# One decode step of cached attention with a gated unit: another order of the weight loads, and the key and value loads of the last pair in one piece

## The chip, the cores and the metric

The kernel runs on one core of a Trainium2 chip. The metric is the device time of one execution in microseconds; lower is better. Before the change the median of three runs is 687.23 us.

## The reference

Everything is float32. One token `x` of 512 elements is normalised, goes through an attention over 8192 cached positions with 32 heads of 128, and the result is multiplied by a gate made from the same normalised token:

```python
def _A_ref(x, k_cache, v_cache, wq, wo):
    q = (lambda x, *d: x.transpose(*d))((x @ wq).reshape(B, Sq, H, Dh), 0, 2, 1, 3)
    scores = jnp.einsum("bhqd,bhkd->bhqk", q, k_cache) * (Dh ** -0.5)
    p = _softmax(scores, axis=-1)
    o = jnp.einsum("bhqk,bhkd->bhqd", p, v_cache)
    return (lambda x, *d: x.transpose(*d))(o, 0, 2, 1, 3).reshape(B, Sq, H * Dh) @ wo
...
    g = jnp.einsum("bsd,df->bsf", x, w_gate)
    u = jnp.einsum("bsd,df->bsf", x, w_up)
    h = _sigmoid(g) * u
    return jnp.einsum("bsf,fd->bsd", h, w_down)
...
    xn = _layernorm(x, axis=-1)
    s = _A_ref(xn, A_k_cache, A_v_cache, A_wq, A_wo)
    g = _silu(_B_ref(xn, B_w_gate, B_w_up, B_w_down))
    return x + s * g
```

`wq` is 512x4096 (8.39 MB), `wo` 4096x512 (8.39 MB), `w_gate` and `w_up` 512x1376 (2.82 MB each), `w_down` 1376x512. The key cache and the value cache have 134 MB each. Every byte is used once, so the kernel is one long load with work beside it.

## The kernel before, in words

Three big buffers hold what is loaded: A, B and C (named slot_55, slot_56 and slot_57 in the built program, slot in the profile), each 128 partitions of 64 KB. The heads go in 16 pairs; the 64 upper partitions carry one head of a pair, the 64 lower ones the other. The keys of pair n, called Kn here, go to B for even n and to A for odd n. The values Vn go to C, except V15, which goes to B. One such load is 8.39 MB, with one row of 64 KB for each partition.

SP issues all the big loads, in the order of its program, and waits on semaphores between them. At the start (L145 to L153) come the gate weights, the up weights and the down weights into A, the last 96 rows of the down weights into `wd_rest`, the query weights into C, and K0 into B. ScalarE issues two small loads: `x_col`, the token as 128 rows of 16 bytes (L148), and `x_row` (L163).

Once `x_col` has landed, VectorE makes the normalised token `xn` (L185 to L199; two small matmuls on TensorE and a square root on ScalarE stand in between). Then, for the gate weights and after them the up weights (loop L211), VectorE multiplies the four slices with `xn` and adds them up (`weighted`, L203), and TensorE sums over the partitions and turns the result by 11 narrow matmuls (L216, L217); this is called a turn below. VectorE multiplies both (L224), does the same with the down weights (L227, L229), and TensorE sums them in four gate matmuls (L233), whose count is `n_gate`. ScalarE and VectorE make the gate row of it (L237, L239). VectorE then spreads `xn` into `xnb` (L240), which lies in the same memory as `wd_rest`, and TensorE computes the queries: eight tiles of four matmuls each, a loop of its own (L246 to L250), one tile to each of the eight PSUM banks; ScalarE copies each to `q_all` (L257).

From there on, for each pair: VectorE multiplies the keys with the query in place and reduces (`scores`, two halves, L277 and L279), the maximum goes through TensorE, ScalarE takes the exponentials into `prz` (`softmax`), and TensorE multiplies them with the values in 64 matmul records once these have landed (`pair`, L314). The waits of SP set when a load may start:

```python
    sp.wait_ge(s_pe.sem, n_gate)
    load_k(1)
...
    sp.wait_ge(s_q, nq)
    for n in range(NP - 1):
        if n:
            sp.wait_ge(s_po, n)
        sp.dma_start(C, rows_of(v_src, n)).then_inc(d_v, 16)
        if n + 2 < NP:
            sp.wait_ge(s_dve.sem, k_free[n])
```

So K1 (into A) waits for the gate matmuls, V0 (into C) for the last query tile, a later Vn for the matmuls with the values before it, and K(n+2) for the scores of pair n. K15 is loaded in two halves (L265), and so is V15 (L342, L343); `pair` waits for the second half of V15 in the middle of its matmuls. At the end `wo` goes to C in five pieces (L346), and TensorE projects (L364 to L389).

Of the kernel before, what the change touches and what calls it, by code (L numbers as in the profile page):

```python
# [9 lines left out]
P = 128  # L10
# [15 lines left out]
def kernel(  # L26
# [11 lines left out]
    nc = tc.nc  # L38
# [31 lines left out]

    A, B, C = (over(f"slot{i}", SLOT, SLOTS + i * SLOT * 4) for i in range(3))
    q_all = put("q_all", NP * Dh).rearrange("p (n d) -> p n d", d=Dh)
    wd_rest = put("o1", QT)
    o1 = wd_rest
    sc = [put("sc0", NB), put("sc1", NB)]
    ident = put("ident", P)
    ones = put("ones", P)
    prz = put("prz", NB * 2).rearrange("p (j a) -> p j a", a=2)
    x_row = put("x_row", GC)
    g_row = put("g_row", GC)  # L80
    heads = put("heads", NP * 4).rearrange("p (n c) -> p n c", c=4)
# [19 lines left out]
    wd_t = A[:, 2 * KT * F:2 * KT * F + FP * D].rearrange("p (r e) -> p r e", e=D)  # L101
    wq_t = C.rearrange("p (k c) -> p k c", k=KT)
    wo_t = C.rearrange("p (r e) -> p r e", e=D)
    late = SLOT // 2

    psum = nc.alloc_psum_tensor("psum", [P, 8 * QT], F32).ap()
    bank = [psum[:, i * QT:(i + 1) * QT] for i in range(8)]
    po, pt, pm, acc, fold_ps, o_ps, oTl = bank[0], bank[1], bank[2], bank[4], bank[5], bank[6], bank[7]


    sems = []
# [24 lines left out]
    k_sem = lambda n: d[f"k{n % 2}"]  # L136
    k_free = {}

    def rows_of(src, n, lo=0, hi=SLOT):
        return src[n * P:(n + 1) * P, lo:hi]  # L140


    xv = x.rearrange("a b d -> (a b d)")
    with tc.tile_critical(no_gpsimd_drain=True):
        d["wg"].by(sp.dma_start(wg_t, w_gate.rearrange("(p k) f -> p k f", k=KT)), 16)  # L145
    tc.close()
    tc.compile()
    d["x"].by(act.dma_start(x_col, xv.rearrange("(p k) -> p k", k=KT)), 16)  # L148
    d["wu"].by(sp.dma_start(wu_t, w_up.rearrange("(p k) f -> p k f", k=KT)), 16)
    d["wd"].by(sp.dma_start(wd_t, w_down[:FP * P, :].rearrange("(p r) e -> p r e", r=FP)), 16)  # L150
    d["wd"].by(sp.dma_start(wd_rest[:FL, :], w_down[FP * P:, :]), 16)
    d["wq"].by(sp.dma_start(wq_t, wq.rearrange("(p k) c -> p k c", k=KT)), 16)
    d["k0"].by(sp.dma_start(B, rows_of(k_src, 0)), 16)  # L153


# [5 lines left out]
    n_xrow = s_dve.by(dve.memset(ones, 1.0))  # L161
    act.wait_ge(s_dve.sem, n_xrow)
    d["xr"].by(act.dma_start(x_row[0:P:GP, :], xv.rearrange("(g c) -> g c", g=NG)), 16)  # L163
    dve.memset(st[:, 6:7], EPS)
    dve.memset(rs2, 0.0)
    dve.memset(prz.rearrange("p j a -> p (j a)"), 0.0)
    for b in (0, 5):
        dve.memset(bank[b], 0.0)
    for b, cols in ((1, GC), (4, GC), (6, FP + 1), (7, FP + 1)):
        dve.memset(bank[b][:, :cols], 0.0)  # L170
    dve.wait_ge(s_pool.sem, 2)
    for g in range(NG):
        n_set = s_dve.by(dve.tensor_copy(pick[g * GP:(g + 1) * GP, :], ident[g * GP:(g + 1) * GP, g * GP:g * GP + ROWS * 2]))
# [2 lines left out]
    def self_wait():  # L176
        dve.wait_ge(s_dve.sem, s_dve.n)
# [28 lines left out]
            self_wait()  # L206
            s_dve.by(dve.scalar_tensor_tensor(acc, t(k), col(k), acc, op0=ALU.mult, op1=ALU.add))  # L207

    turned = [bank[6 + a][:, :FP + 1] for a in range(2)]
    self_wait()  # L210
    for a, (name, t) in enumerate((("wg", wg_t), ("wu", wu_t))):  # L211
        dve.wait_ge(d[name].sem, 16)
        weighted(t[:, 0, :], lambda k: t[:, k, :], lambda k: xn[:, k:k + 1], KT)
        pe.wait_ge(s_dve.sem, s_dve.n)
        for i in range(FP):
            m = pe.matmul(turned[a][:, i:i + 1], t[:, 0, i:FP * P:FP], ones[:, 0:1], start=True, stop=True)  # L216
        m = pe.matmul(turned[a][:FL, FP:FP + 1], t[:, 0, FP * P:F], ones[:, 0:1], start=True, stop=True)  # L217
        n = s_pe.by(m)
        if a == 0:
            act.wait_ge(s_pe.sem, n)  # L220
            n_sg = s_act.by(act.activation(sg, turned[0], AF.Sigmoid))
    dve.wait_ge(s_act.sem, n_sg)
    dve.wait_ge(s_pe.sem, n)
    s_dve.by(dve.tensor_mul(hid, sg, turned[1]))  # L224
    self_wait()
    dve.wait_ge(d["wd"].sem, 32)
    weighted(wd_t[:, 0, :], lambda r: wd_t[:, r, :], lambda r: hid[:, r:r + 1], FP)  # L227
    self_wait()
    s_dve.by(dve.scalar_tensor_tensor(wd_t[:FL, 0, :], wd_rest[:FL, :], hid[:FL, FP:FP + 1], wd_t[:FL, 0, :],  # L229
                                      op0=ALU.mult, op1=ALU.add))  # L230
    pe.wait_ge(s_dve.sem, s_dve.n)
    for g in range(NG):
        m = pe.matmul(bank[1][g * GP:g * GP + 1, :GC], ones[:, 0:1], wd_t[:, 0, g * GC:(g + 1) * GC],  # L233
                      start=True, stop=True)
    n_gate = s_pe.by(m)
    act.wait_ge(s_pe.sem, n_gate)
    n = s_act.by(act.activation(g_row, bank[1][:, :GC], AF.Sigmoid))  # L237
    dve.wait_ge(s_act.sem, n)
    n_grow = s_dve.by(dve.tensor_mul(g_row, g_row, bank[1][:, :GC]))  # L239
    n_xnb = s_dve.by(dve.tensor_copy(xnb, xn.rearrange("p (k o) -> p k o", o=1).to_broadcast([P, KT, P])))  # L240


    pe.wait_ge(d["wq"].sem, 16)
    pe.wait_ge(s_dve.sem, n_xnb)
    nq = H // NG
    with nc.Fori(0, nq, engines=[pe.engine]) as t:  # L246
        for k in range(KT):
            m = pe.matmul(psum[:, bass.ds(t * QT, QT)], xnb[:, k, :], wq_t[:, k, bass.ds(t * QT, QT)],  # L248
                          start=(k == 0), stop=(k == KT - 1))
        m.then_inc(s_q, 1)  # L250
    n_qc = []
    for t in range(nq):
        act.wait_ge(s_q, t + 1)
        pairs = slice(t * NG // 2, (t + 1) * NG // 2)
        for a in range(2):
            r = slice(a * HALF, (a + 1) * HALF)
            c = act.copy(q_all[r, pairs, :], bank[t][r, :].rearrange("p (n a d) -> p n a d", a=2, d=Dh)[:, :, a, :])  # L257
        n_qc.append(s_act.by(c))


    def load_k(n, parts=1):
        w = SLOT // parts
        for i in range(parts):
            c = k_sem(n) if i == parts - 1 else d["ka"]
            c.by(sp.dma_start(k_slot(n)[:, i * w:(i + 1) * w], rows_of(k_src, n, i * w, (i + 1) * w)), 16)  # L265


    def scores(n, waits):
        kt = k_slot(n).rearrange("p (j d) -> p j d", d=Dh)
        s = sc[n % 2]  # L270
        h = NB // 2
        q = q_all[:, n:n + 1, :].to_broadcast([P, h, Dh])
        for i in range(2):
            if waits[i] is not None:
                dve.wait_ge(*waits[i])
            part = kt[:, i * h:(i + 1) * h, :]
            s_dve.by(dve.tensor_mul(part, part, q))  # L277
# [21 lines left out]
        s_act.by(act.copy(heads[:, n, :], oTl[:, 0:4]))  # L299


    def pair(v, waits):
        take(pe, s_rm)
        pe.matmul(pt[:1, :P], mx[:, 0:1], ident, start=True, stop=True).then_inc(s_pt, 1)  # L304
        take(pe, s_am)
        pe.matmul(pm[:, 0:2], ones[:1, :], mx[:1, 2:4], start=True, stop=True).then_inc(s_pm, 1)  # L306
        take(pe, s_pr)
        pe.matmul(oTl[:, 2:4], ones, rs2, start=True, stop=True)  # L308
        nj = NB // ROWS
        for j in range(nj):  # L310
# [3 lines left out]
            m = pe.matmul(po[g * GP:g * GP + 2 * ROWS, :], prz[:, j * ROWS:(j + 1) * ROWS, :],  # L314
                          v[:, j * QT:(j + 1) * QT], start=(j < NG), stop=(j >= nj - NG))
        m.then_inc(s_po, 1)
        take(pe, s_o1)
        for b in range(ROWS):
            m = pe.matmul(oTl[:, 0:2], o1[:, b * Dh:(b + 1) * Dh], pick[:, 2 * b:2 * b + 2],  # L319
                          start=(b == 0), stop=(b == ROWS - 1))  # L320
        m.then_inc(s_ot, 1)
# [3 lines left out]
    for n in range(NP):  # L325
        if n % (NG // 2) == 0:
            dve.wait_ge(s_act.sem, n_qc[n // (NG // 2)])
        if n < NP - 1:
            scores(n, ((k_sem(n).sem, 16 * (n // 2 + 1)), None))
        else:  # L330
            scores(n, ((d["ka"].sem, 16), (k_sem(n).sem, 16 * (n // 2 + 1))))
        softmax(n)
    sp.wait_ge(s_q, nq)
    for n in range(NP - 1):
# [2 lines left out]
        sp.dma_start(C, rows_of(v_src, n)).then_inc(d_v, 16)  # L337
# [5 lines left out]
    d["vb"].by(sp.dma_start(B[:, late:], rows_of(v_src, NP - 1, late, SLOT)), 16)  # L343
# [87 lines left out]
```

## Time and profile before

| | |
|---|---|
| three runs | 687.17, 687.23, 688.38 us |
| the profiled execution, own time | 686.93 us |
| its span, first to last instruction | 685.0 us |
| VectorE busy | 588.8 us (86%) |
| TensorE matmul busy | 241.1 us (35%) |
| ScalarE busy | 41.5 us (6%) |
| read from memory | 293.67 MB |

The profiled execution's time is 1.9 us more than its span, and 0.3 us under the median of the runs. In the profile PE is TensorE, PEld its weight loads, DVE VectorE, ACT ScalarE, POOL GpSimd, SP SyncE; a q behind a name stands for that engine's sequencer. q1 is the DMA queue that SP issues to, q10 the one of ScalarE. L numbers are lines of the kernel before. A matmul in float32 leaves two records, so that 11 matmuls are 22 of them.

### The profile page before, as it was taken

The numbers are of one execution on the slowest core, as the hardware profiler recorded it, in microseconds if no ns is written. First come the engines' busy times: TensorE is split into PE (matmuls) and PEld (weight loads), VectorE is DVE, ScalarE is ACT, GpSimd is POOL, SyncE is SP. The second block draws the span as 40 slices with busy tenths as digits, with TensorE's granted clock in tenths as the row PEclk, the third lists the DMA queues.
The fourth block names the chain that finished last, engine by engine and source line by source line (L and its number), as shares of the span: only waits on it lengthen the run. The fifth ranks groups of instructions, "written<-read, shape, count | busy, mean of one in ns | idle before, by whom it ended". The sixth has DMA issues, their size and how long they took to land. (4 is left out here: it accounts for less than half of the span.)

```text
span 685.0 us, 3539 instructions
## 1 busy us (share of the span) xinstructions
PE 241.1 (35%) x1490; PEld 90.4 (13%) x1490; DVE 588.8 (86%) x147; ACT 41.5 (6%) x135; POOL 0.7 (0%) x6
## 2 busy tenths in 40 slices
PE   0549306060503305050422406060422406060465
PEld 0514101010101101010110101010110101010022
DVE  2643999999999999999989899898979899899930
ACT  1002010000000000000010100000010100000010
POOL 0000000000000000000000000000000000000000
PEclk9999756575665657575565657565565756565689
DMA  9999999999999999999999999999999999999997
GB/s 365 435 429 429 438 425 444 440 432 436 437 432 432 432 429 429 436 444 436 432 436 436 432 432 432 429 429 436 444 436 432 436 436 432 432 419 442 423 430 313
DMA packets 6469, 293.74 MB, mean 429 GB/s; under 512 B 856, under 2 KB 864, under 8 KB 1216
## 3 DMA queue, kind: packets, MB, share of 16 engines
q1 hardware_dynamic: 6312, 293.67, 99.3%
q8 instruction: 3, 0.05, 0.0%
q10 hardware_dynamic: 152, 0.00, 0.0%
q14 instruction: 2, 0.02, 0.0%
HBM read 293.67 MB, written 0.00 MB: 429 GB/s over the span
## 5 line engine op out<-in xcount | busy, mean ns | idle before, releaser
L277 DVE TENSOR_TENSOR slot<-slot,q_all 128x8192 f32<-128x8192 f32 x32 | 277.8, 8681 | 36.7 <-DMA slot<-in_A_k_cache_dram 36.7
L279 DVE TENSOR_REDUCE sc<-slot 128x64 f32<-128x8192 f32 x32 | 278.0, 8686 | 1.1
L314 PE MATMUL psum<-slot,prz 128*8 128x512 f32 x1024 | 147.6, 741 | 214.1 <-PEq L131 214.1
L314 PEld LDWEIGHTS psum<-slot,prz 128*8 128x8 f32 x1024 | 30.1, 103 | 317.9 <-issue 317.9
L304 PE MATMUL psum<-ident,mx 128*1 128x128 f32 x32 | 9.1, 387 | 147.7 <-PEq L131 147.7
L297 ACT COPY o<-psum 128x512 f32<-128x512 f32 x16 | 9.4, 586 | 373.9 <-PE psum L314 373.9
L248 PE MATMUL psum<-slot,o 128*128 x64 | 30.4, 639 | 1.4 <-DVE o L240 1.4
L304 PEld LDWEIGHTS psum<-ident,mx 128*1 128x1 f32 x32 | 1.8, 80 | 149.3 <-issue 149.3
L319 PE MATMUL psum<-pick,o 128*128 128x2 f32 x128 | 16.4, 250 | 12.8 <-PEq L131 12.8
L319 PEld LDWEIGHTS psum<-pick,o 128*128 128x128 f32 x128 | 15.5, 191 | 27.2 <-issue 27.2
L308 PE MATMUL psum<-rs,ones 128*128 128x2 f32 x32 | 8.9, 349 | 23.4 <-PEq L131 23.4
L248 PEld LDWEIGHTS psum<-slot,o 128*128 128x128 f32 x64 | 13.0, 206 | 18.4 <-issue 18.4
L284 DVE TENSOR_REDUCE mx<-psum 1x2 f32<-1x128 f32 x16 | 4.4, 278 | 12.1 <-PE psum L304 12.1
L293 ACT ACTIVATE prz<-sc,mx 64x128 f32<-64x128 f32 x32 | 13.0, 407 | 0.7
L289 ACT ACTIVATE mx<-psum 128x2 f32<-128x2 f32 x16 | 2.8, 172 | 169.9 <-PE psum L306 169.9
L216 PE MATMUL psum<-ones,slot 128*128 128x1 f32 x40 | 9.4, 366 | 7.7 <-DVE slot L207 7.7
L358 DVE RECIPROCAL heads<-heads 128x32 f32<-128x32 f32 x1 | 0.4, 353 | 13.6 <-ACT heads L299 13.6
L306 PE MATMUL psum<-mx,ones 1*128 1x2 f32 x32 | 8.8, 343 | 7.4 <-PEq L131 7.4
L308 PEld LDWEIGHTS psum<-rs,ones 128*128 128x128 f32 x32 | 8.0, 311 | 24.3 <-issue 24.3
L216 PEld LDWEIGHTS psum<-ones,slot 128*128 128x128 f32 x40 | 9.2, 321 | 7.9 <-DVE slot L207 7.9
L207 DVE SCALAR_TENSOR_TENSOR slot<-slot,xn 128x1376 f32<-128x1376 f32 x6 | 9.9, 1652 | 0.2
L306 PEld LDWEIGHTS psum<-mx,ones 1*128 1x128 f32 x32 | 7.9, 305 | 14.7 <-issue 14.7
(59 smaller groups left out, 57.3 us busy)
## 6 DMA issues: line engine op xcount, KB each, us to landing
slot<-in_A_k_cache_dram SPq DMA_DIRECT2D x2, 4096.0 KB, 37.5
slot<-in_A_v_cache_dram SPq DMA_DIRECT2D x2, 4096.0 KB, 37.4
slot<-in_A_wo_dram SPq DMA_DIRECT2D x1, 4096.0 KB, 20.1
slot<-in_B_w_gate_dram SPq DMA_DIRECT2D x1, 2752.0 KB, 9.6
slot<-in_B_w_up_dram SPq DMA_DIRECT2D x1, 2752.0 KB, 14.8
slot<-in_B_w_down_dram SPq DMA_DIRECT2D x1, 2560.0 KB, 20.4
slot<-in_A_wo_dram SPq DMA_DIRECT2D x1, 2048.0 KB, 24.6
slot<-in_A_wo_dram SPq DMA_DIRECT2D x1, 1280.0 KB, 27.1
```

The lines of the kernel that those rows point to most:

```text
L207: s_dve.by(dve.scalar_tensor_tensor(acc, t(k), col(k), acc, op0=ALU.mult, op1=ALU.add))
L216: m = pe.matmul(turned[a][:, i:i + 1], t[:, 0, i:FP * P:FP], ones[:, 0:1], start=True, stop=True)
L248: m = pe.matmul(psum[:, bass.ds(t * QT, QT)], xnb[:, k, :], wq_t[:, k, bass.ds(t * QT, QT)], start=(k == 0), stop=(k == KT - 1))
L277: s_dve.by(dve.tensor_mul(part, part, q))
L279: s_dve.by(dve.reduce_sum(s[:, i * h:(i + 1) * h], part, axis=AX.X))
L293: e = act.activation(prz[r, :, a], sc[n % 2][r, :], AF.Exp, bias=mx[r, 4 + a:5 + a], scale=SCALE, accum_out=rs2[r, a:a + 1])
L297: act.copy(o1, po).then_inc(s_o1, 1)
L304: pe.matmul(pt[:1, :P], mx[:, 0:1], ident, start=True, stop=True).then_inc(s_pt, 1)
L306: pe.matmul(pm[:, 0:2], ones[:1, :], mx[:1, 2:4], start=True, stop=True).then_inc(s_pm, 1)
L308: pe.matmul(oTl[:, 2:4], ones, rs2, start=True, stop=True)
L314: m = pe.matmul(po[g * GP:g * GP + 2 * ROWS, :], prz[:, j * ROWS:(j + 1) * ROWS, :], v[:, j * QT:(j + 1) * QT], start=(j < NG), stop=(j >= ...
L319: m = pe.matmul(oTl[:, 0:2], o1[:, b * Dh:(b + 1) * Dh], pick[:, 2 * b:2 * b + 2], start=(b == 0), stop=(b == ROWS - 1))
```

## The change

The query weights are now the first load on SP's queue, into C; gate, up and down weights follow, then K0. The 96 rows of the down weights go to ScalarE's queue behind `x_row`, with a semaphore of their own, and lie over `sc0`, `sc1` and `prz` and no longer over `xnb`. `prz` is therefore cleared after the down weights are used, on GpSimd. `xnb` is made as soon as `xn` is there, and the query loop is split: tiles 0 to 3 come ahead of the gate's turn, tiles 4 to 7 behind the up turn, ahead of the gate matmuls. The turns use banks 0 and 1 after ScalarE has copied the queries out of these, and the gate matmuls bank 3. The gate row's last multiplication moves behind the scores of pair 0. The memsets of PSUM go away. K15 and V15 are loaded whole. The waits of SP are the same: K1 for `n_gate`, V0 for the last query tile.

```diff
+    o1 = put("o1", QT)
+    wd_rest = over("wd_rest", D, small[0])
...
     with tc.tile_critical(no_gpsimd_drain=True):
-        d["wg"].by(sp.dma_start(wg_t, w_gate.rearrange("(p k) f -> p k f", k=KT)), 16)
+        d["wq"].by(sp.dma_start(wq_t, wq.rearrange("(p k) c -> p k c", k=KT)), 16)
     tc.close()
     tc.compile()
     d["x"].by(act.dma_start(x_col, xv.rearrange("(p k) -> p k", k=KT)), 16)
+    d["wg"].by(sp.dma_start(wg_t, w_gate.rearrange("(p k) f -> p k f", k=KT)), 16)
     d["wu"].by(sp.dma_start(wu_t, w_up.rearrange("(p k) f -> p k f", k=KT)), 16)
     d["wd"].by(sp.dma_start(wd_t, w_down[:FP * P, :].rearrange("(p r) e -> p r e", r=FP)), 16)
-    d["wd"].by(sp.dma_start(wd_rest[:FL, :], w_down[FP * P:, :]), 16)
-    d["wq"].by(sp.dma_start(wq_t, wq.rearrange("(p k) c -> p k c", k=KT)), 16)
     d["k0"].by(sp.dma_start(B, rows_of(k_src, 0)), 16)
...
     d["xr"].by(act.dma_start(x_row[0:P:GP, :], xv.rearrange("(g c) -> g c", g=NG)), 16)
+    d["wr"].by(act.dma_start(wd_rest[:FL, :], w_down[FP * P:, :]), 16)
...
-    dve.memset(prz.rearrange("p j a -> p (j a)"), 0.0)
-    for b in (0, 5):
-        dve.memset(bank[b], 0.0)
-    for b, cols in ((1, GC), (4, GC), (6, FP + 1), (7, FP + 1)):
-        dve.memset(bank[b][:, :cols], 0.0)
...
+    self_wait()
+    n_xnb = s_dve.by(dve.tensor_copy(xnb, xn.rearrange("p (k o) -> p k o", o=1).to_broadcast([P, KT, P])))
...
+    def queries(lo, hi):
+        with nc.Fori(lo, hi, engines=[pe.engine]) as t:
...
+    pe.wait_ge(d["wq"].sem, 16)
+    pe.wait_ge(s_dve.sem, n_xnb)
+    queries(0, nq // 2)
+
+    turned = [bank[a][:, :FP + 1] for a in range(2)]
+    pe.wait_ge(s_act.sem, n_qc[1])
     for a, (name, t) in enumerate((("wg", wg_t), ("wu", wu_t))):
...
+    queries(nq // 2, nq)
     dve.wait_ge(s_act.sem, n_sg)
     dve.wait_ge(s_pe.sem, n)
     s_dve.by(dve.tensor_mul(hid, sg, turned[1]))
     self_wait()
-    dve.wait_ge(d["wd"].sem, 32)
+    dve.wait_ge(d["wd"].sem, 16)
     weighted(wd_t[:, 0, :], lambda r: wd_t[:, r, :], lambda r: hid[:, r:r + 1], FP)
     self_wait()
+    dve.wait_ge(d["wr"].sem, 16)
...
-    pe.wait_ge(s_dve.sem, s_dve.n)
+    n_wr = s_dve.n
+    pool.wait_ge(s_dve.sem, n_wr)
+    n_prz = s_pool.by(pool.memset(prz.rearrange("p j a -> p (j a)"), 0.0))
+    act.wait_ge(s_pool.sem, n_prz)
+    pe.wait_ge(s_dve.sem, n_wr)
...
+        scores(n)
+        if n == 0:
+            dve.wait_ge(s_act.sem, n_gs)
+            s_dve.by(dve.tensor_mul(g_row, g_row, g_ps[:, :GC]))
         softmax(n)
...
-            load_k(n + 2, 2 if n + 2 == NP - 1 else 1)
+            load_k(n + 2)
     sp.wait_ge(s_dve.sem, k_free[NP - 2])
-    d["va"].by(sp.dma_start(B[:, :late], rows_of(v_src, NP - 1, 0, late)), 16)
-    d["vb"].by(sp.dma_start(B[:, late:], rows_of(v_src, NP - 1, late, SLOT)), 16)
+    d["va"].by(sp.dma_start(B, rows_of(v_src, NP - 1)), 16)
...
-    pair(B, {0: lambda: pe.wait_ge(d["va"].sem, 16), NB // ROWS // 2: lambda: pe.wait_ge(d["vb"].sem, 16)})
+    pair(B, lambda: pe.wait_ge(d["va"].sem, 16))
```

On TensorE, from the statistics of the token to the first pair, the order before is this; slot_55 is A, slot_57 is C, o_59 is `xnb`. L216 and L217 are the turns, L233 the gate matmuls, L248 the body of the loop over eight query tiles.

```order
L181 MATMUL psum<-st,ones 128x1 x2
L216 MATMUL psum<-ones,slot_55 128x1 x10
L217 MATMUL psum<-ones,slot_55 96x1
L216 MATMUL psum<-ones,slot_55 128x1 x10
L217 MATMUL psum<-ones,slot_55 96x1
L233 MATMUL psum<-slot_55,ones 1x128 x4
L246 UNCONDITIONAL_BRANCH
L246 ISA
L248 MATMUL psum<-slot_57,o_59 128x512
```

And this is the same place now; L213 is the body of the two query loops of four tiles each, L235 and L236 are the turns, L258 the gate matmuls.

```order
L175 MATMUL psum<-st,ones 128x1 x2
L211 UNCONDITIONAL_BRANCH
...
L213 MATMUL psum<-slot_57,o_59 128x512
...
L235 MATMUL psum<-ones,slot_55 128x1 x10
L236 MATMUL psum<-ones,slot_55 96x1
L235 MATMUL psum<-ones,slot_55 128x1 x10
L236 MATMUL psum<-ones,slot_55 96x1
L211 UNCONDITIONAL_BRANCH
...
L213 MATMUL psum<-slot_57,o_59 128x512
...
L258 MATMUL psum<-slot_55,ones 1x128 x4
```

The gate matmuls, which stood ahead of all query tiles, now stand behind all of them, and the turns between the two halves of the queries.

On SP, the first loads before; slot_56 is B.

```order
L145 DMA slot_55<-in_B_w_gate_dram 128x5504
...
L149 DMA slot_55<-in_B_w_up_dram 128x5504
L150 DMA slot_55<-in_B_w_down_dram 128x5120
L151 DMA o_59<-in_B_w_down_dram 96x512
L152 DMA slot_57<-in_A_wq_dram 128x16384
L153 DMA slot_56<-in_A_k_cache_dram 128x16384
L265 DMA slot_55<-in_A_k_cache_dram 128x16384
L337 DMA slot_57<-in_A_v_cache_dram 128x16384
```

And now:

```order
L144 DMA slot_57<-in_A_wq_dram 128x16384
...
L148 DMA slot_55<-in_B_w_gate_dram 128x5504
L149 DMA slot_55<-in_B_w_up_dram 128x5504
L150 DMA slot_55<-in_B_w_down_dram 128x5120
L151 DMA slot_56<-in_A_k_cache_dram 128x16384
L266 DMA slot_55<-in_A_k_cache_dram 128x16384
L336 DMA slot_57<-in_A_v_cache_dram 128x16384
```

The query weights moved from the fifth place to the first, and the 96 rows left this queue; the loads from K0 on stand in the same order as before.

More of the change, by code (lines that the diff above doesn't have):

```diff
@@ L72 @@
     q_all = put("q_all", NP * Dh).rearrange("p (n d) -> p n d", d=Dh)
-    wd_rest = put("o1", QT)
-    o1 = wd_rest
+    o1 = put("o1", QT)
+    wd_rest = over("wd_rest", D, small[0])
     sc = [put("sc0", NB), put("sc1", NB)]
+    prz = put("prz", NB * 2).rearrange("p (j a) -> p j a", a=2)
     ident = put("ident", P)
     ones = put("ones", P)
-    prz = put("prz", NB * 2).rearrange("p (j a) -> p j a", a=2)
     x_row = put("x_row", GC)
@@ L103 @@
     wo_t = C.rearrange("p (r e) -> p r e", e=D)
-    late = SLOT // 2
     psum = nc.alloc_psum_tensor("psum", [P, 8 * QT], F32).ap()
     bank = [psum[:, i * QT:(i + 1) * QT] for i in range(8)]
-    po, pt, pm, acc, fold_ps, o_ps, oTl = bank[0], bank[1], bank[2], bank[4], bank[5], bank[6], bank[7]
+    po, pt, pm, g_ps, acc, fold_ps, o_ps, oTl = bank
     sems = []
@@ L115, in semaphore @@
         return sems[-1]
-    names = "x xr wg wu wd wq ka k0 k1 va vb".split()
+    names = "x xr wg wu wd wr wq k0 k1 va".split()
     d = {n: Count(semaphore(f"d_{n}")) for n in names}
@@ L137, with rows_of @@
     k_free = {}
-    def rows_of(src, n, lo=0, hi=SLOT):
-        return src[n * P:(n + 1) * P, lo:hi]
+    def rows_of(src, n):
+        return src[n * P:(n + 1) * P, :]
     xv = x.rearrange("a b d -> (a b d)")
     with tc.tile_critical(no_gpsimd_drain=True):
-        d["wg"].by(sp.dma_start(wg_t, w_gate.rearrange("(p k) f -> p k f", k=KT)), 16)
+        d["wq"].by(sp.dma_start(wq_t, wq.rearrange("(p k) c -> p k c", k=KT)), 16)
     tc.close()
@@ L207, in weighted @@
             s_dve.by(dve.scalar_tensor_tensor(acc, t(k), col(k), acc, op0=ALU.mult, op1=ALU.add))
-    turned = [bank[6 + a][:, :FP + 1] for a in range(2)]
     self_wait()
+    n_xnb = s_dve.by(dve.tensor_copy(xnb, xn.rearrange("p (k o) -> p k o", o=1).to_broadcast([P, KT, P])))
+    nq = H // NG
+    n_qc = []
+    def queries(lo, hi):
+        with nc.Fori(lo, hi, engines=[pe.engine]) as t:
+            for k in range(KT):
+                m = pe.matmul(psum[:, bass.ds(t * QT, QT)], xnb[:, k, :], wq_t[:, k, bass.ds(t * QT, QT)],
+                              start=(k == 0), stop=(k == KT - 1))
+            m.then_inc(s_q, 1)
+        for t in range(lo, hi):
+            act.wait_ge(s_q, t + 1)
+            pairs = slice(t * NG // 2, (t + 1) * NG // 2)
+            for a in range(2):
+                r = slice(a * HALF, (a + 1) * HALF)
+                c = act.copy(q_all[r, pairs, :], bank[t][r, :].rearrange("p (n a d) -> p n a d", a=2, d=Dh)[:, :, a, :])
+            n_qc.append(s_act.by(c))
+    pe.wait_ge(d["wq"].sem, 16)
[3 more added lines that the diff above has]
+    pe.wait_ge(s_act.sem, n_qc[1])
     for a, (name, t) in enumerate((("wg", wg_t), ("wu", wu_t))):
@@ L225 @@
     self_wait()
-    dve.wait_ge(d["wd"].sem, 32)
+    dve.wait_ge(d["wd"].sem, 16)
     weighted(wd_t[:, 0, :], lambda r: wd_t[:, r, :], lambda r: hid[:, r:r + 1], FP)
     self_wait()
+    dve.wait_ge(d["wr"].sem, 16)
     s_dve.by(dve.scalar_tensor_tensor(wd_t[:FL, 0, :], wd_rest[:FL, :], hid[:FL, FP:FP + 1], wd_t[:FL, 0, :],
                                       op0=ALU.mult, op1=ALU.add))
-    pe.wait_ge(s_dve.sem, s_dve.n)
+    n_wr = s_dve.n
[3 more added lines that the diff above has]
+    pe.wait_ge(s_dve.sem, n_wr)
     for g in range(NG):
-        m = pe.matmul(bank[1][g * GP:g * GP + 1, :GC], ones[:, 0:1], wd_t[:, 0, g * GC:(g + 1) * GC],
+        m = pe.matmul(g_ps[g * GP:g * GP + 1, :GC], ones[:, 0:1], wd_t[:, 0, g * GC:(g + 1) * GC],
                       start=True, stop=True)
@@ L236, with load_k, scores @@
     act.wait_ge(s_pe.sem, n_gate)
[L237 to L268, printed above, removed]
+    n_gs = s_act.by(act.activation(g_row, g_ps[:, :GC], AF.Sigmoid))
+    def load_k(n):
+        k_sem(n).by(sp.dma_start(k_slot(n), rows_of(k_src, n)), 16)
+    def scores(n):
         kt = k_slot(n).rearrange("p (j d) -> p j d", d=Dh)
@@ L272, in scores @@
         q = q_all[:, n:n + 1, :].to_broadcast([P, h, Dh])
+        dve.wait_ge(k_sem(n).sem, 16 * (n // 2 + 1))
         for i in range(2):
-            if waits[i] is not None:
-                dve.wait_ge(*waits[i])
             part = kt[:, i * h:(i + 1) * h, :]
@@ L299, in softmax, with pair @@
         s_act.by(act.copy(heads[:, n, :], oTl[:, 0:4]))
-    def pair(v, waits):
+    def pair(v, landed):
         take(pe, s_rm)
@@ L309, in pair @@
         nj = NB // ROWS
+        landed()
         for j in range(nj):
-            if j in waits:
-                waits[j]()
             g = j % NG
@@ L327 @@
             dve.wait_ge(s_act.sem, n_qc[n // (NG // 2)])
[L328 to L331, printed above, removed]
+        scores(n)
+        if n == 0:
+            dve.wait_ge(s_act.sem, n_gs)
+            s_dve.by(dve.tensor_mul(g_row, g_row, g_ps[:, :GC]))
         softmax(n)
@@ L349 @@
     with nc.Fori(0, NP - 1, engines=[pe.engine], head_slot={pe.engine: 0}):
-        pair(C, {0: lambda: take(pe, d_v, 16)})
-    pair(B, {0: lambda: pe.wait_ge(d["va"].sem, 16), NB // ROWS // 2: lambda: pe.wait_ge(d["vb"].sem, 16)})
+        pair(C, lambda: take(pe, d_v, 16))
+    pair(B, lambda: pe.wait_ge(d["va"].sem, 16))
     turn = A[:, :P]
```

## The prediction

> **What bounds the kernel now.** First the page: its span, the slices of the DMA engines, and the queues.
>
> ```profile
> span 685.0 us, 3539 instructions
> DMA  9999999999999999999999999999999999999997
> GB/s 365 435 429 429 438 425 444 440 432 436 437 432 432 432 429 429 436 444 436 432 436 436 432 432 432 429 429 436 444 436 432 436 436 432 432 419 442 423 430 313
> q1 hardware_dynamic: 6312, 293.67, 99.3%
> ```
>
> The 16 DMA engines are busy in every slice, and 99.3% of their time goes to SP's queue (q1). VectorE is busy for 86%, but not on the path. The DMA queue section asked for 100 to 300 us gives the undisturbed rate:
>
> ```profile
> DMA packets 1505, 87.04 MB, mean 435 GB/s; under 512 B 176, under 2 KB 176, under 8 KB 176
> ```
>
> 293.67 MB at 435 GB/s are 675 us of the 685. The chain that ended last agrees; its longest piece is a load:
>
> ```profile
> 653.12 27.15 DMA slot<-in_A_wo_dram
> ```
>
> So the sum is short: the bytes stay the same, and the change can only alter the stretches in which the queue is empty, which before has only at its ends. SP can issue K1 (keys of pair 1, into A) only after the gate's last matmul, and V0 (into C) only after the last query matmul. SP's own waits show both:
>
> ```profile
> SPq L265 <- PE psum L233: 38.3, 1, 38.3
> SPq L337 <- PE psum L248: 31.4, 1, 31.4
> ```
>
> **The start, in the timeline.** Columns are start, duration, engine and line, operation.
>
> ```profile
> 0.96 0.39 SPq L145 DMA_DIRECT2D slot<-in_B_w_gate_dram  x1
> 2.35 0.39 ACTq L148 DMA_DIRECT2D x_col<-in_A_x_dram  x1
> 13.60 0.16 DVE L185 TENSOR_REDUCE st<-x_col 128x1 f32<-128x4 f32 x1 [8.47 <-DMA x_col<-in_A_x_dram]
> 16.42 0.23 DVE L199 TENSOR_SCALAR xn<-xc,st 128x4 f32<-128x4 f32 x1
> 22.74 4.69 PE L216 MATMUL psum<-ones,slot 128*128 128x1 f32 x20 [6.85 <-DVE slot L207]
> 28.64 4.69 PE L216 MATMUL psum<-ones,slot 128*128 128x1 f32 x20 [0.90 <-DVE slot L207]
> 33.20 0.46 PE L217 MATMUL psum<-ones,slot 128*96 128x1 f32 x2
> 42.38 0.61 PE L233 MATMUL psum<-slot,ones 128*1 128x128 f32 x8 [8.72 <-DVE slot L229]
> 43.04 0.33 SPq L265 DMA_DIRECT2D slot<-in_A_k_cache_dram  x1
> 43.57 0.42 DVE L240 COPY o<-xn 128x512 f32<-128x512 f32 x1
> 44.35 16.20 PE L248 MATMUL psum<-slot,o 128*128 x31 [1.37 <-DVE o L240]
> ```
>
> ```profile
> 61.02 0.75 ACT L257 COPY q_all<-psum 64x256 f32<-64x256 f32 x2 [2.69 <-PE psum L248]
> 62.94 8.69 DVE L277 TENSOR_TENSOR slot<-slot,q_all 128x8192 f32<-128x8192 f32 x1 [18.96 <-DMA slot<-in_A_k_cache_dram]
> 74.74 0.33 SPq L337 DMA_DIRECT2D slot<-in_A_v_cache_dram  x1
> 113.11 1.02 PE L319 MATMUL psum<-pick,o 128*128 128x2 f32 x8 [0.81 <-PEq L131]
> ```
>
> K0 lands at 62.9. K1 was issued at 43.0, 20 us ahead; V0 came at 74.7, before K1's 19.3 us (8.39 MB at 435 GB/s) ran out at 82.2. The queue never ran dry, although TensorE's query loop ended 12 us after K0: it lay behind the gate and held only V0 back.
>
> **The change: K1 now waits for nearly everything on TensorE.** The new order is four query tiles, gate turn, up turn, four query tiles, gate matmuls; K1 waits for the last. I add that chain up, from its first input.
>
> *When x arrives.* The first query tile needs xnb, hence x_col, on ScalarE's queue (q10). The DMA issues, then the queues' packets up to 6.2 us, then from 6.2 to 13.6 us:
>
> ```profile
> slot<-in_B_w_gate_dram SPq DMA_DIRECT2D x1, 2752.0 KB, 9.6
> slot<-in_B_w_down_dram SPq DMA_DIRECT2D x1, 2560.0 KB, 20.4
> x_col<-in_A_x_dram ACTq DMA_DIRECT2D x1, 2.0 KB, 11.2
> ```
>
> ```profile
> q1 hardware_dynamic: 72, 1.59, 72.5%
> ...
> q1 hardware_dynamic: 158, 3.13, 98.7%
> q10 hardware_dynamic: 148, 0.00, 1.2%
> ```
>
> While x_col runs, the two queues' packets come nearly one for one (158 and 148): an engine serves one row of SP's load, then one 16-byte row of x_col. Before, SP's rows are the gate's, 22 KB or 0.81 us each (27.2 GB/s per engine). x_col has 128 rows and 16 semaphore writes, nine turns per engine, 7.3 us: 6.2 to 13.5, as seen. It lands at 13.55, 3.0 us or 3.6 gate rows behind the gate's own landing (0.96 + 9.6 = 10.56).
>
> In the change the first load is the query weights, 64 KB a row, 2.41 us a turn, eight rows per engine. Before, 8.26 MB (gate, up, down) had landed at 2.73 + 20.4 = 23.1; 8.39 MB land at about 23.4. x_col's turns now outlast these eight rows and end among the gate's. If it enters after as many rows as before (72 / 16 = 4.5), it again lands 3.6 gate rows behind the first load, at 26.3; if it enters after a fixed time (6.2 us, two of the long rows), 1.1 rows behind, at 24.3. I take 26.0, nearer to the count, which a queue of started rows would give.
>
> [...]
>
> *From x to the first query matmul.* 13.60 to 16.65 for the statistics (L185 to the end of L199), 0.8 from the start of the copy to the first matmul (43.57 to 44.35): 3.9 us. The removed memsets (L166 to L170) lay inside VectorE's 8.47 us wait for x_col and give nothing. Matmuls start at 29.9.
>
> *Queries 0 to 3.* Before, four tiles took 44.35 to 61.02, 16.7 us, the other four 61.02 to 74.74, 13.7 us: the loop starts at half clock. 46.6.
>
> *The two turns (22 matmul records each).* VectorE has weighted the gate's rows by 36 (they land near 30; then 6 us, as from 16.7 to 22.7) and the up rows by 42.5, so both turns wait for TensorE alone. Before, a turn took 5.0 us (28.64 to 33.66). At full clock the nearest row is L319, also 128x128 weights and few columns: 8 records in 1.02 us, so 2.8 us for 22. How long does the clock stay up? The stretches after the query loop, with the granted clock third from the end:
>
> ```profile
> 72.00:76.00 4.00, 2.71 (x7) 0.93 (x5) 4.00 (x1) 0.80 (x3) 0.00 (x0) 1.00 0.79 344
> 76.00:80.00 4.00, 0.00 (x0) 0.00 (x0) 4.00 (x1) 0.00 (x0) 0.00 (x0) 0.62 1.10 475
> ```
>
> 0.62 over four microseconds is about one at full clock and three at half: it fell at 77, 2.2 us after the loop. [...] So the first turn runs fast and the second slow: 2.8 + 5.0 = 7.8 us. Bounds: 5.6 and 10.0. 54.4.
>
> *Queries 4 to 7.* From half clock again: 16.7 (bound 13.7). 71.1. VectorE's down rows, 8.7 us from the up turn's end to the gate matmuls (33.66 to 42.38), end at 63, hidden.
>
> *Gate matmuls and K1.* 0.66 us (42.38 to 43.04): K1 is issued at 71.8.
>
> *What that costs.* A first load pays a start: the gate's 2.82 MB need 6.5 us at 435 GB/s and landed after 9.6, so 3.1 us. K0 still lands at 62.9, as the bytes ahead of it are the same. An unbroken queue would deliver K1 19.3 us after K0, now it does 3.1 + 19.3 after its issue: 71.8 + 3.1 - 62.9 = **12.0 us** of empty queue. It starts to cost when K1 is issued after 59.8. Nothing gives it back: every later load lies behind it on a full queue. VectorE's scores of pair 0 end at 97.7 as before and K1 is there at 94.2, so no second gap opens.
>
> *The end.* V15 is loaded whole. The last pair, in the timeline and in the landing of V15's second half:
>
> ```profile
> 620.49 0.43 SPq L343 DMA_DIRECT2D slot<-in_A_v_cache_dram  x1
> 621.39 8.67 DVE L277 TENSOR_TENSOR slot<-slot,q_all 128x8192 f32<-128x8192 f32 x1
> 643.39 8.82 PE L314 MATMUL psum<-slot,prz 128*8 128x512 f32 x64 [19.30 <-PEq L131]
> 659.82 9.14 PE L314 MATMUL psum<-slot,prz 128*8 128x512 f32 x64
> 677.26 1.90 PE L376 MATMUL psum<-slot,o_all 128*1 128x512 f32 x16 [1.06 <-DMA slot<-in_A_wo_dram]
> 680.32 1.27 PE L380 MATMUL psum<-slot,o_all 128*1 128x128 f32 x40 [1.15 <-DMA slot<-in_A_wo_dram]
> ```
>
> ```profile
> DMA to landing us min/median/max: 42.1/42.1/42.1
> ```
>
> V15's second half lands at 620.49 + 42.1 = 662.6; TensorE started on the first at 659.82. Now it waits 2.8 us longer. K15 whole hides inside that: V14 landed at 643.4, so K15 at 624, VectorE starts 2.6 us later than 621.39, and its weights are ready by 662.4. Behind V15 lie waits for wo of 1.06 and 1.15 us that swallow 2.2 of the 2.8. I take **0.5 us** (0 to 2). Down rows on ScalarE's queue: same bytes, same engines, needed at 62; nothing. The gate product moved behind the first scores, 0.3 us on VectorE, is covered by its waits for keys; the prz memset by TensorE's loop. Merging the halves saves two issues of 0.4 us on a queue that is ahead: nothing.
>
> **Sum.** 12.0 + 0.5 = 12.5 us on the profiled execution's 686.93 gives 699.4; the median of the runs is 0.3 higher, so **699.7**. A difference under 0.2% (1.4 us) can't be told from none.
>
> **Rivals.**
>
> *x_col early (10%).* If it is served in few turns, matmuls start on the query weights at 23.5; 40.2, first turn 43.0, second 48.0, queries 64.7, K1 at 65.4. Gap 5.6, with the end 693.3. Against it: the one-for-one count.
>
> *The clock holds through the turns (15%).* 29.9 + 16.7 + 5.6 + 13.7 + 0.4: K1 at 66.3, gap 6.5, 694.2. [...]
>
> *Not slower (7%).* K1's release falls before 59.8: x early and the clock held give 23.5 + 16.7 + 5.6 + 13.7 + 0.4 = 59.9, the very edge. Then the queue stays full: 687.7 with the end, or 687.2 if the end hides too. It needs both rivals at once; 2% of it I leave for faster by 1.4 us, for which no empty stretch exists to be filled but the start and the end.
>
> *Forecast (68%).* Its own range: x at 24.3 to 26.9, turns 5.6 to 10.0, K1 at 68 to 75. The low bounds all together (24.3, 5.6, 13.7) give K1 at 64.6 and 692.5; the high ones 74.9 and, with the end's 2, 704. The range 692.5 to 703.5 takes in the first two rivals. Slower 0.93, same 0.05, faster 0.02.
>
> **What would show it.** K1's issue near 72 with SP waiting for the gate matmuls; DMA share near zero for some 10 us around 63 to 73; x_col landing behind the query weights, at 24 to 27; the second query loop's first tile at half clock; V15's matmuls starting on its landing. Wrong if K1 is issued before 60 or if x_col lands near 13.

## The result, and the profile after

The changed kernel takes 698.48 us (median of six runs, 696.99 to 701.44) against 687.57 us (six runs, 687.17 to 688.38): 10.9 us slower by the medians, and a ratio over all runs of 1.0163, 95% interval 1.0134 to 1.0191. The runs lie in two groups, three at 697.0 and three from 699.9 to 701.4; the kernel before has nothing of the kind. The profiled execution is one of the first group, 697.02 us. In the experiments below two runs, at 705.15 us (everything but the order) and at 700.55 (both edits, and halves), are in a slow state and are left out of the medians and ratios.

The page of the changed kernel, its span, DMA slices and SP's queue:

```profile
span 695.1 us, 3534 instructions
DMA  9994999999999999999999999999999999999997
GB/s 392 402 465 192 420 422 422 426 457 441 427 422 426 434 456 434 422 426 426 460 437 422 426 422 464 437 422 426 422 464 434 426 426 422 464 434 426 426 420 307
q1 hardware_dynamic: 5912, 293.47, 97.8%
```

One slice besides the last is not full: the fourth, 52 to 70 us, at 192 GB/s. The stretches 60 to 64 and 64 to 68 us show the hole itself; the last two columns are DMA share and GB/s:

```profile
60.00:64.00 4.00, 4.00 (x11) 1.82 (x10) 3.04 (x3) 0.74 (x3) 0.31 (x1) 1.00 0.00 0
64.00:68.00 4.00, 4.00 (x10) 1.71 (x9) 4.00 (x1) 0.73 (x2) 0.00 (x0) 1.00 0.00 0
```

TensorE is busy in both stretches from end to end. SP's waits name the wait that took 38.3 us before:

```profile
SPq L266 <- PE psum L258: 65.7, 1, 65.7
```

The start in the timeline, where before the gate matmuls stood at 42.38 and K1's issue at 43.04:

```profile
23.71 0.16 DVE L179 TENSOR_REDUCE st<-x_col 128x1 f32<-128x4 f32 x1 [19.86 <-DMA x_col<-in_A_x_dram]
27.62 15.78 PE L213 MATMUL psum<-slot,o 128*128 x32 [1.62 <-DVE o L204]
43.24 4.47 PE L235 MATMUL psum<-ones,slot 128*128 128x1 f32 x20
47.74 4.66 PE L235 MATMUL psum<-ones,slot 128*128 128x1 f32 x20
52.58 16.94 PE L213 MATMUL psum<-slot,o 128*128 x32
62.32 8.69 DVE L277 TENSOR_TENSOR slot<-slot,q_all 128x8192 f32<-128x8192 f32 x1 [0.93 <-DMA slot<-in_A_k_cache_dram]
69.45 0.40 PE L258 MATMUL psum<-slot,ones 128*1 128x128 f32 x8
69.91 0.33 SPq L266 DMA_DIRECT2D slot<-in_A_k_cache_dram  x1
```

K0 is there at 62.3 (its last bytes had moved by 60, as the empty stretch shows), and K1 is not issued until 69.9. From issue to landing K1 took this long, before and after:

```profile
slot<-in_A_k_cache_dram SPq DMA_DIRECT2D x1, 40.2
```

```profile
slot<-in_A_k_cache_dram SPq DMA_DIRECT2D x1, 23.2
```

So K1 landed at 43.0 + 40.2 = 83.2 before and at 69.9 + 23.2 = 93.1 now: 9.9 us later. The difference of the two profiled spans is 10.1. In this execution nearly all of the loss is the hole; the executions at 700 and above lose something more, which the experiments look for.

### The profile page after: what moved, and what is told of

Same layout as the page of the kernel before. It is cut to its first block, busy times and chain, and to the rows that moved or that the text cites. A ratio compares the mean times of both kernels' runs of the same rounds, so it can differ in the third digit from the quotient of the medians.

```text
span 695.1 us, 3534 instructions
## 1 busy us (share of the span) xinstructions
PE 241.8 (35%) x1490; PEld 91.0 (13%) x1490; DVE 587.8 (85%) x140; ACT 41.4 (6%) x135; POOL 1.0 (0%) x7
## 5 line engine op out<-in xcount | busy, mean ns | idle before, releaser
L313 PE MATMUL psum<-slot,prz 128*8 128x512 f32 x1024 | 146.9, 738 | 272.2 <-PEq L130 272.2
L313 PEld LDWEIGHTS psum<-slot,prz 128*8 128x8 f32 x1024 | 30.1, 103 | 375.5 <-issue 375.4
L213 PE MATMUL psum<-slot,o 128*128 x64 | 32.7, 676 | 1.6 <-DVE o L204 1.6
L318 PE MATMUL psum<-pick,o 128*128 128x2 f32 x128 | 16.4, 250 | 12.8 <-PEq L130 12.8
L318 PEld LDWEIGHTS psum<-pick,o 128*128 128x128 f32 x128 | 15.5, 191 | 27.2 <-issue 27.2
L213 PEld LDWEIGHTS psum<-slot,o 128*128 128x128 f32 x64 | 13.8, 220 | 19.0 <-issue 19.0
L308 PEld LDWEIGHTS psum<-rs,ones 128*128 128x128 f32 x32 | 8.0, 312 | 24.3 <-issue 24.3
L175 PE MATMUL psum<-st,ones 128*128 128x1 f32 x4 | 1.2, 362 | 24.8 <-DVE st L179 23.9
```

## The experiments

Each kernel has one profiled execution and a median over its runs; lines left out of a diff are marked by three dots. Beside each median stands its difference from the kernel before on the same chip. The first four were timed together, then the next four, then the last four.

**x_col ahead of the query weights.**

```diff
     with tc.tile_critical(no_gpsimd_drain=True):
+        d["x"].by(sp.dma_start(x_col, xv.rearrange("(p k) -> p k", k=KT)), 16)
         d["wq"].by(sp.dma_start(wq_t, wq.rearrange("(p k) c -> p k c", k=KT)), 16)
...
-    d["x"].by(act.dma_start(x_col, xv.rearrange("(p k) -> p k", k=KT)), 16)
```

> The changed kernel with x_col issued by SP ahead of the query weights, so that it waits for none of their rows. Theory (K1 is held by TensorE's chain, and the chain starts late because x_col takes turns with the 64 KB rows): x_col lands near 3 to 5 us, the first query matmul starts at the query weights' landing, about 23.5 instead of 27.6, K1 is issued near 65.6 instead of 69.9, and the time falls by about 4.3 us to 694. It should also scatter less between executions, if the scatter of the changed kernel comes from x_col. Rival (the time is lost elsewhere, in the two queues sharing the engines, or at the end behind V15): the time stays at 697 to 701.

697.53 us (695.09 to 697.97), 9.9 over the kernel before, where the changed kernel in the same company was 12.8 over. Its timeline:

```profile
25.49 16.28 PE L213 MATMUL psum<-slot,o 128*128 x32 [18.84 <-DMA slot<-in_A_wq_dram]
66.84 0.33 SPq L266 DMA_DIRECT2D slot<-in_A_k_cache_dram  x1
68.00 8.69 DVE L277 TENSOR_TENSOR slot<-slot,q_all 128x8192 f32<-128x8192 f32 x1 [8.23 <-DMA slot<-in_A_k_cache_dram]
669.43 9.91 PE L313 MATMUL psum<-slot,prz 128*8 128x512 f32 x64
683.20 8.13 PE L374 MATMUL psum<-slot,o_all 128*1 128x512 f32 x48 [0.28 <-DVE o_all L364]
```

TensorE now waits for the query weights and not for x, and K1 is issued 3.1 us earlier. The size fell short of the 4.3 us expected, since the weights landed 2.3 us later than before the edit, at 25.2 and not 22.9; in the kernel with both edits they land at 24.6. In this one profiled execution the first loads ran slowly throughout (K0 at 68.0, where all others have it between 62.3 and 63.1), which no other kernel repeats; why is open. What K1 gained reached the end of the kernel: the matmuls with V15 (L313) start at 669.43, 3.3 us earlier than the 672.68 of the changed kernel. From there to the end of the span, however, this execution took 26.4 us and the changed kernel's first 22.4, so its span (695.8) is no shorter. The run of the changed kernel again, below, shows what that depends on. The medians of the two kernels in the same company differ by 3.0 us.

**The gate matmuls ahead of query tiles 4 to 7.**

```diff
-    queries(nq // 2, nq)
     dve.wait_ge(s_act.sem, n_sg)
...
     n_gs = s_act.by(act.activation(g_row, g_ps[:, :GC], AF.Sigmoid))
+    queries(nq // 2, nq)
```

> The changed kernel with the gate matmuls ahead of query tiles 4 to 7, and x_col left late. Theory: K1 is issued when VectorE is done with the down weights, near 62, the gap in the load queue shrinks from about 10 to 2 us, and the time is about 689. V0 waits for the last tile at about 78.5, before K1 has run out at 85, and costs nothing. Rival (loss elsewhere): 697 to 701. Rival (V0, now 8 us later, opens a gap of its own): above 692.

692.94 us (689.46 to 694.42), 5.3 over before. K1 and V0 were issued here:

```profile
63.65 0.33 SPq L266 DMA_DIRECT2D slot<-in_A_k_cache_dram  x1
79.67 0.33 SPq L336 DMA_DIRECT2D slot<-in_A_v_cache_dram  x1
```

K1 comes 6.3 us earlier than in the changed kernel and the time falls by 7.5, so the place of the gate matmuls held it for about two thirds of the hole. V0's own lateness opened nothing: K1 landed at 86.9. But the median is 4 us above the 689 expected, and only the fastest run reaches it. The executions scatter over 5 us, and the profiled one, the slowest, lost the time at its end: its matmuls with V15 start at 666.19, 6.5 us earlier than in the changed kernel, but from there to the end it took 26.3 us and not 22.4.

**Both edits.**

> Both edits: x_col first and the gate matmuls ahead of query tiles 4 to 7. Theory: K1 is issued near 58, before the 59.8 from which it costs, the queue never runs dry, and what is left of the change is its end (0.1 to 0.5 us): 687.5 to 688.0. Rival (loss elsewhere): well above 690.

689.52 us (twelve runs, 687.11 to 691.67), 1.9 over before. K1 is issued at the edge from which a gap was to cost:

```profile
59.25 0.33 SPq L266 DMA_DIRECT2D slot<-in_A_k_cache_dram  x1
62.94 8.69 DVE L277 TENSOR_TENSOR slot<-slot,q_all 128x8192 f32<-128x8192 f32 x1 [4.41 <-DMA slot<-in_A_k_cache_dram]
```

The hole is gone, and the fastest runs equal the kernel before; half of the twelve are at 690.4 or above. The median misses the 687.5 to 688.0 expected. What is left is not the start.

**The changed kernel again, unedited.**

> The changed kernel once more, unedited, for the scatter of its times (three of its executions near 697.0, three from 699.9 to 701.4). Theory: the scatter is x_col, which takes a few more turns in some executions; a profiled execution near 700 or above would show it landing 3 or 4 us later than 23.7, one near 697 at 23.7. Rival: the scatter is the clock of TensorE's loops, with x_col at 23.7 in every execution.

700.49 us (five runs, 699.04 to 701.29), 12.8 over before. The profiled execution is one of 699.04, and VectorE took up x_col in it at 23.9, against 23.7 in the one of 697.02: the theory's account of the scatter fell. The two differ at the end. The timelines, first of the execution of 697.02, then of that of 699.04, with the projection at L374:

```profile
672.68 8.86 PE L313 MATMUL psum<-slot,prz 128*8 128x512 f32 x64
685.17 5.33 PE L374 MATMUL psum<-slot,o_all 128*1 128x512 f32 x48 [0.28 <-DVE o_all L364]
```

```profile
673.36 8.70 PE L313 MATMUL psum<-slot,prz 128*8 128x512 f32 x64
685.69 7.03 PE L374 MATMUL psum<-slot,o_all 128*1 128x512 f32 x48 [0.28 <-DVE o_all L364]
```

And a stretch in the projection of each, in the same order, with the granted clock third from the end:

```profile
684.00:688.00 4.00, 3.24 (x30) 1.02 (x34) 0.58 (x3) 0.00 (x0) 0.00 (x0) 1.00 0.99 420
```

```profile
686.00:690.00 4.00, 4.00 (x28) 0.87 (x24) 0.00 (x0) 0.00 (x0) 0.00 (x0) 0.62 0.97 411
```

The same 48 records took 5.33 us with the clock at 1.00 and 7.03 where it read 0.62. Between the end of the matmuls with V15 and the projection lie 3.6 us in both, of which TensorE is busy for 1.4 (its lines L318 and L362); the clock reads 1.00 from 680 to 692 us in the first, and 1.00 from 682 to 686 and then the 0.62 in the second. In the slowest run of the second experiment, the profiled one of 694.42, the records took 8.13; there the clock reads 0.73 from 677 to 681 us, ahead of and at the start of the projection, and 0.50 in the stretch from 681 us:

```profile
679.96 8.13 PE L374 MATMUL psum<-slot,o_all 128*1 128x512 f32 x48 [0.28 <-DVE o_all L364]
```

```profile
681.00:685.00 4.00, 4.00 (x20) 0.58 (x16) 0.00 (x0) 0.00 (x0) 0.00 (x0) 0.50 0.77 313
```

So the rival held, with a correction: it is the clock, but at the end and not in the query loops. The profiled executions of all the kernels agree. Where K15, V15 or both are loaded whole, the time from the start of the matmuls with V15 to the end of the span is 22.3 to 22.5 us in the six in which the projection took 5.33, 23.8 in the three in which it took 7.03, and 26.3 and 26.4 in the two in which it took 8.13. That makes 4 us, nearly as much as the changed kernel scatters. Where both are in halves it is 25.2 or 25.3, whatever the clock. That the runs without a profile scatter for the same reason is inferred.

**Half rows for the query weights.**

```diff
-        d["wq"].by(sp.dma_start(wq_t, wq.rearrange("(p k) c -> p k c", k=KT)), 16)
+        wq_s = wq.rearrange("(p k) c -> p k c", k=KT)
+        for i in range(2):
+            d["wq"].by(sp.dma_start(wq_t[:, 2 * i:2 * i + 2, :], wq_s[:, 2 * i:2 * i + 2, :]), 16)
...
-    pe.wait_ge(d["wq"].sem, 16)
+    pe.wait_ge(d["wq"].sem, 32)
```

> The changed kernel with the query weights loaded by two DMAs of half rows (32 KB each), same bytes, same place in the queue. If an engine gives x_col one turn for each row of SP's load, its nine turns last half as long: it lands between 15 and 20 us, ahead of the query weights, the first query matmul starts near 23.5 and the time falls by about 4 us to 694. If x_col simply waits until the whole first load is through, whatever its rows, nothing changes: x_col at about 23.7 and 697 to 701.

696.80 us (695.47 to 697.26), 9.2 over before. Its timeline:

```profile
16.90 0.16 DVE L181 TENSOR_REDUCE st<-x_col 128x1 f32<-128x4 f32 x1 [12.58 <-DMA x_col<-in_A_x_dram]
24.05 15.96 PE L215 MATMUL psum<-slot,o 128*128 x32 [4.87 <-DMA slot<-in_A_wq_dram]
66.62 0.33 SPq L268 DMA_DIRECT2D slot<-in_A_k_cache_dram  x1
```

x_col lands at 16.9 instead of 23.7 with nothing changed but the length of SP's rows, inside the 15 to 20 of the theory of turns, and K1 follows 3.3 us earlier. That it merely waits for the whole load is refuted. The median lies 2.8 us above the 694 expected; in the profiled execution, 695.47, the projection took 7.03 us.

**The turns' weights from neighbouring columns.**

```diff
-            m = pe.matmul(turned[a][:, i:i + 1], t[:, 0, i:FP * P:FP], ones[:, 0:1], start=True, stop=True)
+            m = pe.matmul(turned[a][:, i:i + 1], t[:, 0, i * P:(i + 1) * P], ones[:, 0:1], start=True, stop=True)
```

> The changed kernel with the turns reading their weights from neighbouring columns and not from every tenth; the hidden vector is then in another order than the down weights expect, so this computes a different gate and only its time counts. If the first turn is slow (4.8 us at full clock where 2.8 were forecast) because of the step of ten, it falls to 2.8 us and the second to between 2.8 and 5.0: K1 2 to 4 us earlier, 693 to 695. If the turns are slow for another reason, the time stays at 697 to 701.

692.60 us (691.51 to 695.16), 5.0 over before. The turns and K1:

```profile
43.75 2.29 PE L235 MATMUL psum<-ones,slot 128*128 128x1 f32 x20
46.07 2.37 PE L235 MATMUL psum<-ones,slot 128*128 128x1 f32 x20
64.54 0.33 SPq L266 DMA_DIRECT2D slot<-in_A_k_cache_dram  x1
```

Both turns halve, 4.47 and 4.66 to 2.29 and 2.37, and K1 comes 5.4 us earlier, more than the 2 to 4 expected. The step of ten columns is what made the first turn slow in the changed kernel, 4.47 us with the clock at 1.00. The rest of the gain is in the queries behind the turns, which take 15.7 us and not 16.9: their weight loads follow each other every 0.85 us from 49.6 to 52.2 us and every 0.43 from 52.8 on, where the changed kernel has 0.85 from 53.6 to 57.8, with the clock at 0.50 from 52 to 56.

**The last pair whole, and nothing else** (the kernel before with the two edits of the diff at `load_k` and V15).

> The kernel before, with only K15 and V15 loaded whole. Theory: the last matmuls with the values wait for the whole of V15, 2.8 us later, and the waits for wo swallow nearly all: 0.1 to 0.5 us more than before, 687.6 to 688.0. Rival (the end is where the change loses): 690 or more.

689.67 us (twelve runs, 686.68 to 691.19), 2.1 over before; ratio 1.0025, interval 1.0013 to 1.0038, which is 1.7 us. The theory's 0.1 to 0.5 is too small. The runs again lie in two groups, five up to 687.62 and seven from 689.34: whole loads alone bring both the loss and the scatter.

**Everything but the order** (that, with the 96 rows on ScalarE's queue, `prz` cleared on GpSimd and fewer memsets, in the order of before).

> The kernel before with everything of the change but the order: last pair whole, the 96 rows on ScalarE's queue and away from xnb, prz cleared on GpSimd, fewer memsets. Loads, turns, gate and queries stay in the order of before. Theory: as with the whole last pair alone, 687.6 to 688.0, since K1 is issued near 43 again. Rival (the two queues sharing the engines cost time): 689 or more.

688.20 us (eleven runs, 687.05 to 690.61), 0.6 over before; ratio 1.0021, interval 1.0009 to 1.0033. Where runs lie in two groups the median jumps with a run or two; by the ratio this is no more than the last pair alone costs, so the second queue costs nothing that shows.

**The order alone** (the changed kernel with K15 and V15 in halves).

> The changed kernel with K15 and V15 loaded in halves again, so that the new order alone is left. First theory (the gap at K1 and the end are two separate losses, 10 us and 0 to 4 us, and the scatter of the changed kernel belongs to the end): 687.6 plus 9.9 gives 697.5, and the executions lie within 1.5 us. Rival (the scatter and some of the loss belong to the new order): it scatters over 3 us or more, as the changed kernel does, with a median near 700.

697.42 us (696.99 to 698.04), 10.2 over before. Its end:

```profile
683.02 7.03 PE L385 MATMUL psum<-slot,o_all 128*1 128x512 f32 x48 [0.98 <-DMA slot<-in_A_wo_dram]
690.82 1.27 PE L389 MATMUL psum<-slot,o_all 128*1 128x128 f32 x40 [0.78 <-DMA slot<-in_A_wo_dram]
```

The scatter is gone, as far as four runs show, and the time is 687.25 plus the 9.9 of the hole, within 0.3. Here too the clock fell (0.67 from 682 to 686 us) and the projection took 7.03 us, but TensorE still had to wait for wo, so it cost nothing. That separates the two losses.

**Both edits, and halves** (x_col first, gate matmuls early, last pair in halves).

> The changed kernel with x_col first, the gate matmuls ahead of query tiles 4 to 7, and the last pair in halves. First theory: both losses are gone, 687.3 to 688.0 with executions within 1.5 us, no faster than before because the load queue was full before too. Rival (the order costs something apart from K1's release): 689 or more.

687.47 us (ten runs, 687.13 to 688.47), 0.2 over before, ratio 1.0006 with an interval of 0.9997 to 1.0015. Its projection took 7.03 us as well, behind a wait for wo of 0.54, and cost nothing. Nothing of the loss is left, and nothing is gained.

**K15 alone whole, V15 alone whole.**

> The kernel before with K15 alone loaded whole. First theory (the last matmuls with the values start 2.6 us later because VectorE starts later, and this alone uses up the slack of TensorE's closing chain): scatter of some 3 us upwards, median 688.5 to 690. Rival (K15 costs nothing, since V15's landing sets the start): 687.6 with no scatter.

> The kernel before with V15 alone loaded whole. First theory (the last matmuls with the values start 2.8 us later, at V15's landing, and TensorE's closing chain then meets its slow clock): scatter of some 3 us upwards, median 689 to 690. Rival (V15 costs nothing of its own): 687.6 with no scatter.

K15 alone: 689.09 us (687.07 to 690.75), 1.8 over before, interval 1.0014 to 1.0039. V15 alone: 687.99 us (686.84 to 690.50), 0.7 over, interval 1.0003 to 1.0025. The matmuls with V15 in the two:

```profile
662.43 8.62 PE L314 MATMUL psum<-slot,prz 128*8 128x512 f32 x64
```

```profile
662.72 8.97 PE L314 MATMUL psum<-slot,prz 128*8 128x512 f32 x64 [2.49 <-DMA slot<-in_A_v_cache_dram]
```

Either one starts them 2.6 to 2.9 us later than the 659.82 of before, by another cause: VectorE's late start on K15 (623.76 where before has 621.39) or V15's landing. Both scatter upwards. V15's median stayed below the 689 to 690 expected; whether it is really cheaper than K15 or the twelve runs fell out so is open, the intervals overlap.

## Why the prediction was right

Forecast were 699.7 us and a hole of 12.0 us before K1 with 0.5 us at the end. Measured: about 10 in the hole (9.9 between the traces, 10.2 for the order alone) and about 2 at the end (the last pair alone: 2.1 by the medians, 1.7 by the ratio), with 10.9 for both in the first six runs and 12.8 in the five later ones. The cause, its place and the sign were right; that the total came so near is luck in part, because one term was too large and another too small.

*K1 behind the gate, the gate behind everything.* Forecast at 71.8, issued at 69.9. Moving the gate matmuls alone brought K1 forward by 6.3 us, and moving them with x_col removed the hole.

*When x arrives.* Forecast 26.0, landed 23.7; the other end, 24.3, for x_col entering after a fixed time and not after a count of rows, was nearer. The turns themselves are as described, one small packet for each long row. The queues' packets from 12 to 16 us:

```profile
q1 hardware_dynamic: 32, 2.10, 121.8%
q10 hardware_dynamic: 32, 0.00, 0.4%
```

The rival by which x_col is through early is refuted by this.

*Queries.* Forecast 16.7 for each half; the first four tiles took 15.2 until the turn began (27.62 to 42.8), the other four 16.9. The column of the granted clock shows nothing of the first loop's slow start: it reads 1.00 from 20 us on, while the first few weight loads follow each other every 0.85 us and those after 31 us every 0.43. Nor does it in the kernel before, where it reads 1.00 from 44 to 76 us and the first four tiles took 16.7 us, the others 13.7; that this loop starts at half clock was read from its times alone. In the changed kernel the column's first fall stands at 48 us. The second half did begin at half clock, as forecast, so the rival with a held clock fell; the granted clock during the turns:

```profile
44.00:48.00 4.00, 4.00 (x21) 4.00 (x20) 0.00 (x0) 1.55 (x3) 0.00 (x0) 1.00 1.21 524
48.00:52.00 4.00, 4.00 (x19) 4.00 (x20) 0.00 (x0) 0.09 (x1) 0.00 (x0) 0.54 0.94 410
```

It fell from 1.00 to 0.54 while TensorE was busy with turns without a break, and read 0.50 in the next stretch, 52 to 56 us.

*The turns.* One step that failed: "At full clock the nearest row is L319 [...] so 2.8 us for 22". The first turn took 4.8 us with the clock at 1.00. L319 reads its weights from neighbouring columns, the turn from every tenth, and with neighbouring columns the turn took 2.6. The two turns were 2 us longer than forecast. That the first would be fast and the second slow, 2.8 and 5.0 us, no run shows: their batches of 20 records took 4.47 us and 4.66, with the clock at 1.00 and 0.54. The equal batches of before, 4.69 us each, told nothing of the clock, which reads 1.00 there from 20 to 36 us.

*What K1's issue costs.* The unbroken queue delivered K1 20.4 us after K0 (62.8 to 83.2), not 19.3, and K1 took 23.2 after its issue, not 22.4. With the issue 1.9 us earlier that makes 9.9 for 12.0.

*The end.* The other step that failed: "Behind V15 lie waits for wo of 1.06 and 1.15 us that swallow 2.2 of the 2.8. I take 0.5 us". The late start of 2.8 us was right, and the profiled execution did lose only some 0.2. Its matmuls with V15 start within 0.1 us of V15's landing, but show no wait for it: VectorE's late start on K15, which the prediction took to hide inside that wait, sets the same moment. But the forecast carried over the closing chain's times from an execution in which the clock stayed up during the projection:

```profile
674.00:678.00 4.00, 2.94 (x32) 0.52 (x24) 0.00 (x0) 0.00 (x0) 0.00 (x0) 1.00 1.00 424
```

The waits for wo were also what hid a projection at a lower clock. A projection of 7.03 us cost nothing where the halves are kept and 1.4 us where they are not (23.8 us against 22.4 for the whole end); with 8.13 the end was 4 us longer. I had given 0 to 2 for this; the runs show 0 to nearly 4.

## What to carry to other kernels

Where the load queue is the bound, ask of each load which instruction releases it and put that instruction as early as its engine allows; the gate matmuls took 0.4 us, and standing behind 17 us of queries cost 6 of the 10 us of the hole. The 16-byte rows of x_col on the second queue came one for one with the 64 KB rows of the first (32 and 32 packets from 12 to 16 us), and it landed 21.3 us after its issue; issued ahead of that big load on the same queue it landed after 1.6. So try a tiny input that is needed early ahead of the big load. And slack at the end of a chain is worth more than one profile shows: the projection here took 5.33 us with the clock at 1.00 in one execution and 8.13 in another, with it at 0.50 from 681 to 685 us, so look at the scatter of the times before calling the slack spare.

## What the runs showed of the hardware

A load of 128 rows of 16 bytes took 21.3 us from its issue to its landing beside rows of 64 KB on the other queue, 14.1 beside rows of 32 KB, 11.2 beside the 22 KB of the kernel before, and 1.6 when it was issued first on the same queue as the 64 KB rows. Turns with float32 weights of 128 columns took 0.22 us a record with a step of ten columns and the clock at 1.00 (4.47 us for 20), 0.11 without the step (2.29 for 20). The granted clock went from 1.00 (44 to 48 us) to 0.54 (48 to 52 us) while TensorE ran nothing but matmuls with one column each, without a break. At the end of the kernel it read 0.73 from 677 to 681 us and 0.50 from 681 to 685 where 48 records of the projection took 8.13 us (the gate matmuls moved alone), 0.62 from 686 to 690 where they took 7.03 (the changed kernel again), and 1.00 from 684 to 692 where they took 5.33 (the changed kernel).
